# Attention and MLP on one core: batch 0 loaded in 1 KB pieces, queries kept in piece order, batch 1 loaded whole ahead of the weights

## The chip, the cores and the metric

The kernel runs on one core of a Trainium2 chip. The metric is the time of one execution on the device in microseconds (us). TensorE (PE), VectorE (DVE), ScalarE (ACT) and GpSimd (POOL) each have a queue of instructions of their own that they work off in order; SyncE (SP) here only issues DMA transfers. A DMA can also be issued from ScalarE's or GpSimd's queue, and then takes a place in that queue.

## The reference

```python
B, H, S, D = 8, 8, 576, 64
scores = scale * q @ k.T                      # per batch and head
cum = cumsum(maximum(s, 0.0))                 # per batch and head, over S
bias = minimum(-(cum[query] - cum[key]), 0.0)
scores = where(causal, -1e9, scores + bias)   # causal: key after query
attn = softmax(scores);  x = attn @ v         # x: [B, S, 512], the heads side by side
xn = (x - mean(x)) / sqrt(var(x) + 1e-6) * g_ln
out = x + maximum(xn @ w_ch1, 0.0) @ w_ch2    # 512 -> 2048 -> 512, all float32
```

## The kernel before

**Tiling.** The 576 tokens of a batch make four full blocks of 128 and a tail of 64 (`NF` = 4, `NT` = 5, `TL` = 64). A head's scores are computed transposed: keys on the partitions, queries along the row, one block of keys after the other and only the queries from that block on (`score_mms`). Blocks 0 and 1 go to the PSUM tile `s01`, blocks 2 and 3 to `s23`, block 4 to the end of the tile `pot`, of which there are two. ScalarE takes the exponential into `e` (`score_exp`); `values` multiplies `e` with V and a column of ones into `pot`, and VectorE divides by the sums into `x` (L272, L273). The causal mask is added by a matmul with `negm` for the first 12 heads (`NPM`), and applied by GpSimd to `e` after that (L236).

**Bias.** The cumulative sum enters the score matmul as four more rows of the contraction: `aug` holds, per token and head, 64 values of q or k, then the sum split into bf16 parts (`split`, `shift`). The sum is computed with tokens along the row and transposed by TensorE into `c8` (L502 to L508; `cum_quads` for batches in `QUADS`).

**Loads.** Batches 0 to 2 are loaded head by head in float32 (`head_in`, 128 KB each) into `homes`: those of q and k of batch 1 are `xbufs[0]`, where the cumulative sum is computed first, and the place of batch 0's q; that of v of batch 1 is the place of batch 0's k. A head is cast to bf16 into `aug` or `v_bf` (`cast_head`, called by `feed` four heads ahead), which frees its place. In batches of `QUADS` (1 and 2) partition p receives tokens 4p to 4p + 3 of q and k as one piece of 1 KB; in batch 0, and for v, a piece is one token of 256 bytes. The last 64 tokens of several heads come in one transfer (`tails_in`). From batch 3 on, `loads` brings token blocks through a ring.

**Transposes.** `t_pe` turns `aug` into `qkT` (68 rows, tokens along the row) by TensorE through PSUM tiles `pt`; `ps_m` has three such buffers, shared with the MLP's `ph` and `py`. For `QUADS`, `t_quads` transposes the pieces, and the copy from PSUM to `qkT` puts the tokens back into their order (L170 to L174), the tails of q and k in one copy of 128 after both (L175). From batch 3 on DMA transposes do this work.

**MLP.** When a batch is done, `stats`, `norm` and `x_t` normalize it, and `chunk_units` adds 32 units of work: 16 times up (4 matmuls into `ph`, ReLU into `hT` on ScalarE or VectorE) and 16 times down (4 matmuls; each fourth finishes 128 tokens of `py`, VectorE adds `x` into `yo`, and `store` puts the tile on the list `late`). `mlp(n)` runs up to n units; ahead of each it issues the stores of all tiles but the last on ScalarE's queue (L303). `yo` has two buffers.

**Order.** The program is written out for heads g = 0 to 63 in a loop of fixed places: "a", scores, "a2", exponentials and MLP units, "b", values of head g - 1, "x", "c", "d", "e". `at(g, place, f)` hangs work onto a place. The first MLP units run at head 11. W1 is loaded by four transfers on GpSimd's queue at heads 6, 6, 7, 7, W2 at 10, 10, 11, 11, both cast to bf16 on the way. The heads of batch 1 are issued on SP at heads 0, 0, 1, 1, 7, 7, 8, 8, those of batch 2 from head 12 on. `spin` issues matmuls whose result is not used.

Of the kernel before, what the change touches and what calls it, by code (L numbers as in the profile page):

```python
# [9 lines left out]
F32 = mybir.dt.float32  # L10
BF16 = mybir.dt.bfloat16
ALU = mybir.AluOpType
# [4 lines left out]
def kernel(  # L17
# [35 lines left out]

    QUADS = (1, 2)
    NPX = 2
# [17 lines left out]

    negm = const.tile([P, P], BF16, name="negm")
    nc.gpsimd.memset(negm, 0.0)
    nc.gpsimd.affine_select(
        out=negm, in_=negm, compare_op=ALU.is_ge, fill=-131072.0, base=0, pattern=[[1, P]],
        channel_multiplier=-1,
    )

# [16 lines left out]
    xnT_tail = const.tile([P, 2, KD, P], BF16, name="xnT_tail")  # L97

    scr = xbufs[0]
    ident_f = scr[:BH, 4:5, 64 : 64 + BH].rearrange("p a b -> p (a b)")  # L100
# [4 lines left out]

    nc.sync.dma_start(out=s_sb, in_=s.rearrange("b h s -> (b h) s"))


# [12 lines left out]
    def copy(eng, o, i):  # L121
        if eng == "act":
            nc.scalar.copy(out=o, in_=i)
        elif eng == "dve":
            nc.vector.tensor_copy(out=o, in_=i)  # L125
        else:
            nc.gpsimd.tensor_copy(out=o, in_=i)  # L127
# [33 lines left out]
    def t_quads(b, h, engs):  # L161
        pts = [ps_m.tile([P, 2 * 512], BF16, name="pt", tag="pm") for _ in range(2)]
        tails = pts[1][0:DK, NF * P : NF * P + 2 * P].rearrange("r (j n) -> r j n", j=2)
        for i in range(2):
            for p in range(NF):
                nc.tensor.transpose(  # L166
                    pts[i][0:DK, p * P : (p + 1) * P], aug[:, p, i * H + h, 0:DK], ident
                )
            nc.tensor.transpose(tails[:, i, :], aug[:, NF, i * H + h, 0:DK], ident)
            copy(  # L170
                engs[i],
                qkT[b][0:DK, i * H + h, 0 : NF * P].rearrange("r (p t) -> r p t", t=NF),
                pts[i][0:DK, 0 : NF * P].rearrange("r (t p) -> r p t", t=NF),
            )  # L174
        copy(  # L175
            "dve", qkT[b][0:DK, :, NF * P : S].rearrange("r (j h) n -> r j h n", j=2)[:, :, h, :],
            tails[:, :, 0:TL],
        )

    def t_pe(b, h, engs=("dve", "dve")):  # L180
        if b in QUADS:
            return t_quads(b, h, engs)
        for j, eng in ((h, engs[0]), (H + h, engs[1])):
            pt = ps_m.tile([P, 2 * 512], BF16, name="pt", tag="pm")
            for p in range(NT):
                nc.tensor.transpose(pt[0:DK, p * P : (p + 1) * P], aug[:, p, j, 0:DK], ident)
            copy(eng, qkT[b][0:DK, j, :], pt[0:DK, 0:SP_])

# [9 lines left out]
    def score_mms(g):  # L198
        b, h = g // H, g % H
        s01 = ps_s.tile([P, 1024], F32, name="s01", tag="s01")  # L200
        s23 = ps_s.tile([P, 512], F32, name="s23", tag="s23")
        pot = ps_o.tile([P, 512], F32, name="pot", tag="pot")
        pots[g] = (pot, s01, s23)

        def mm(o, kb, lo, hi):
            lhsT = qkT[b][0:DK, H + h, kb * P : (kb + 1) * P]
            w = 0
            if g < NPM and lo == kb * P:
                w = min(P, hi - lo)
                nc.tensor.matmul(  # L210
                    o[:, 0:w], lhsT=lhsT, rhs=qkT[b][0:DK, h, lo : lo + w], start=True, stop=False
                )
                nc.tensor.matmul(
                    o[:, 0:w], lhsT=ident, rhs=negm[:, 0:w], start=False, stop=True
                )
            if lo + w < hi:
                nc.tensor.matmul(  # L217
                    o[:, w:], lhsT=lhsT, rhs=qkT[b][0:DK, h, lo + w : hi], start=True, stop=True
                )

        mm(s01[:, 0:512], 0, 0, 512)
        mm(s01[:, 512:576], 0, 512, 576)
        mm(s01[:, 576:1024], 1, 128, 576)
        mm(s23[:, 0:320], 2, 256, 576)
        mm(s23[:, 320:512], 3, 384, 576)
        mm(pot[:, 448:512], 4, 512, 576)

    def score_exp(g, part):
        pot, s01, s23 = pots[g]
        e = ebufs[g % 3]  # L230

        def ex(o, i):
            nc.scalar.activation(out=o, in_=i, func=ACT.Exp, scale=scale)  # L233

        def mask(d):
            nc.gpsimd.affine_select(  # L236
                out=d, in_=d, compare_op=ALU.is_ge, fill=0.0, base=0,
                pattern=[[0, d.shape[1]], [1, P]], channel_multiplier=-1,
            )

        if part == 0:
            ex(e[:, 0:1024], s01)
        else:
            ex(e[:, EO[2] : EO[2] + 512], s23)
            ex(e[:, EO[4] : EO[4] + TL], pot[:, 448:512])
            if g >= NPM:
                mask(e[:, 0 : 3 * S].rearrange("p (n c) -> p n c", c=S)[:, :, 0:P])
                mask(
                    e[:, EO[4] + P - 448 : EO[3] + P]
                    .rearrange("p (n c) -> p n c", c=448)[:, :, 448 - P : 448]  # L250
                )

# [39 lines left out]
    def store(c, a, yo):  # L292
        if c >= B:
            b0 = 4 * (c - B) + 2 * a
            late.append((out[b0, NF * P : S, :], yo[0:TL]))
            late.append((out[b0 + 1, NF * P : S, :], yo[TL:P]))
        else:
            late.append((out[c, a * P : (a + 1) * P, :], yo))

    def stores(eng, keep=0):  # L300
        while len(late) > keep:
            o, i = late.pop(0)
            eng.dma_start(out=o, in_=i)  # L303

# [185 lines left out]
    def spin(n):  # L490
        for _ in range(n):
            nc.tensor.matmul(idle[:, 0:P], lhsT=ident, rhs=ident, start=True, stop=True)

    spin(44)
    nc.vector.tensor_scalar(
# [5 lines left out]
    )  # L501
    pc = ps_m.tile([P, 512], F32, name="pc", tag="pm")  # L502
    for p in range(NT):
        nc.tensor.transpose(pc[:, p * BH : (p + 1) * BH], cum[:, p * P : (p + 1) * P], ident_f)
    c8, r8 = (
        x[:, 0 : NT * BH].rearrange("p (t c) -> p t c", c=BH) for x in (xts[2], xts[1])
    )
    pc_v = pc[:, 0 : NT * BH].rearrange("p (t c) -> p t c", c=BH)  # L508

# [11 lines left out]
    cast_head("k", 0, 0, "pool")  # L521
    split(0, H, nc.vector, pc_v[:, :, 0:H], aug[:, :, H:HD, D1:DK])
    nc.scalar.activation(
# [3 lines left out]
    cast_head("k", 0, 1, "pool")  # L527
    spin(8)
    t_pe(0, 0, ("act", "dve"))
    nc.scalar.copy(out=c8, in_=pc_v)  # L530

    def cum_quads():

        pq = ps_m.tile([P, 512], F32, name="pq", tag="pm")[:, 0 : NF * 3 * H]
        pq = pq.rearrange("p (t c) -> p t c", t=NF)
        cum_q = cum[0 : 3 * H, 0 : NF * P].rearrange("c (p t) -> c t p", t=NF)
        for p in range(NF):
            nc.tensor.transpose(pq[:, p, :], cum_q[:, p, :], ident_f[0 : 3 * H, 0 : 3 * H])
        qs = slice(QUADS[0] * H, (QUADS[-1] + 1) * H)
        nc.vector.tensor_copy(out=c8[:, 0:NF, qs], in_=pq[:, :, qs])  # L540

# [10 lines left out]
    def at(g, pos, f):  # L552
        hooks.setdefault((g, pos), []).append(f)
# [13 lines left out]
    def t_next(g):  # L567
        t_pe((g + 2) // H, (g + 2) % H, ("dve", "act" if g >= H else "dve"))

    at(0, "a2", lambda: t_pe(0, 1))  # L570
    at(0, "a2", cum_quads)
    at(2, "c", lambda: split(H, 2 * H, nc.vector))
# [3 lines left out]
    for g in range(2 * H):  # L576
        if g < 12:
            at(g, "a", lambda g=g: feed(g))
        if g < 14:
            at(g, "a2" if g < H else "b", lambda g=g: t_next(g))  # L580
    for c, g in enumerate((6, 6, 7, 7)):
        at(g, "a", lambda c=c: load_w1(c))
# [6 lines left out]
    def b1_in(h):  # L589
        if h == 2:  # L590
            nc.sync.dma_start(out=gln_b, in_=moe_g_ln.partition_broadcast(P))
        heads_in(1, (h,))
        if h % HH == 0:
            for what in "qkv":
                tails_in(what, 1, nc.sync, slice(h, h + HH))

    for h, g in enumerate((0, 0, 1, 1, 7, 7, 8, 8)):
        at(g, "e", lambda h=h: b1_in(h))
# [6 lines left out]
    def t_act(b, h):  # L605
        t_pe(b, h, ("dve", "act"))

# [18 lines left out]
    at(10, "c", lambda: chunk_units(0))  # L626
    for i, g in enumerate((10, 10, 11, 11)):
        at(g, "b", lambda i=i: load_w2(i))
    for p in (1, 2, 3, 4):
        at(6 + p, "e", lambda p=p: nc.gpsimd.memset(aug[:, p, :, DK:P], 0.0))  # L630


    def b2_in(g):
        if g == 12:
            for what in "qkv":
                tails_in(what, 2, nc.sync)
        heads_in(2, range(3 * (g - 12), min(H, 3 * (g - 12) + 3)))

    for g in (12, 13, 14):
        at(g, "a", lambda g=g: b2_in(g))  # L640
# [62 lines left out]
    for g in range(NG + 4):  # L703
# [7 lines left out]
        if g < NG:  # L711
            score_mms(g)
            run(g, "a2")
            score_exp(g, 0)
        mlp(min(1, nu))
# [44 lines left out]
```

The softmax here doesn't subtract the row's maximum and nothing guards it: scores larger than these inputs give would overflow.

## Time and profile before

| what | value |
|---|---|
| median of 13 runs | 378.66 us |
| lowest, highest | 377.45, 381.04 us |
| profiled execution: its own time | 378.0 us |
| profiled execution: span of its instructions | 376.3 us |
| granted TensorE clock | 0.999 |
| bytes moved by DMA | 59.12 MB |
| first MLP matmul (`ph`) starts at | 42.9 us |
| exponential of head 0, 8, 16 starts at | 10.4, 30.2, 80.3 us |

The profile is that of one execution, 0.66 us below the median. Times inside it count from the start of the span. A group's row names the line, engine, operation, output and input with their shapes, and the count, then the busy time in us and the mean of one in ns, then the idle time of the engine just before and what ended it. A row of the waits names the waiting work, what ended the wait, the total in us, how often, and the longest.

### The profile page before, as it was taken

To read this page: it belongs to the slowest core of one execution; us is meant where nothing else is said; L and a number is where in the kernel's file an instruction comes from. 1 tells how busy PE (TensorE), PEld (TensorE's weight loads), DVE (VectorE), ACT (ScalarE), POOL (GpSimd) and SP (SyncE) were. 2 spreads that over 40 slices of the span, in tenths; PEclk is the share of its full clock that TensorE was granted. 3 is DMA by queue.
4 is the path that set the end of the run, shared out by engine and by line. 5 is a ranking of instruction groups with operands and counts; after the bars stand their busy time and mean duration, and the time that the engine had idled before them with its cause. 6 is when DMAs were issued, how large, how long until landed. Compare 5 with 4: busy or idle time off the path is not lost.

```text
span 376.3 us, 7905 instructions
## 1 busy us (share of the span) xinstructions
PE 352.6 (94%) x2991; PEld 204.1 (54%) x3017; DVE 200.7 (53%) x466; ACT 164.1 (44%) x295; POOL 167.8 (45%) x328
## 2 busy tenths in 40 slices
PE   7977879798999999999999999999999999899994
PEld 6866545365555455555555755555555555344471
DVE  6789565754455434594447335723555453933131
ACT  3666665154651476336632546434633563031020
POOL 3647973592635546475446444463444111600000
PEclk9999999999999999999999999999999999999999
DMA  9978989997999399999999999699604001420202
GB/s 164 212 187 183 216 146 207 247 240 158 209 217 250 83 213 204 228 207 195 191 200 254 178 246 212 128 214 214 118 28 113 29 2 56 113 56 0 86 28 56
DMA packets 175254, 59.12 MB, mean 157 GB/s; under 512 B 162225, under 2 KB 170417, under 8 KB 175217
## 3 DMA queue, kind: packets, MB, share of 16 engines
q1 hardware_dynamic: 165200, 46.43, 64.1%
q0 software_dynamic: 4224, 4.19, 6.9%
q10 hardware_dynamic: 5792, 8.00, 6.4%
q8 instruction: 23, 0.38, 0.4%
q14 instruction: 15, 0.11, 0.1%
HBM read 37.11 MB, written 9.44 MB: 124 GB/s over the span
## 4 chain that ended last, share of the span: by engine, by line
PE 74%; DMA 10%; DVE 6%; SPq 4%; issue 2%; POOL 1%; ACT 1%; POOLq 0%; DVEq 0%; ACTq 0%
PE ph L373 29%; PE py L384 27%; PE s L217 9%; PE pot L264 6%; DMA ring<-in_k_dram 4%; DMA ring<-in_q_dram 4%; SPq L430 2%; DVE xn L323 2%; DVE stats L308 1%; SPq L434 1%; DMA xnT<-xn 1%; SPq L422 1%; DVE x L273 1%; PE pt L166 1%; DMA out_dram<-yo 1%
## 5 line engine op out<-in xcount | busy, mean ns | idle before, releaser
L233 ACT ACTIVATE e<-s 128x1024 bf16<-128x1024 f32 (+1 forms) x128 | 99.1, 808 | 87.4 <-PE s L217 83.8
L384 PE MATMUL py<-w_bf,hT 128*128 128x512 bf16 x550 | 129.8, 379 | 1.4
L373 PE MATMUL ph<-xnT,w_bf 128*128 128x512 bf16 x512 | 120.7, 379 | 1.7 <-DMA xnT<-xn 1.7
L236 POOL TENSOR_SCALAR_AFFINE_SELECT e<-e 128x384 bf16<-128x384 bf16 x104 | 45.9, 466 | 111.2 <-ACT e L233 102.7
L358 DVE TENSOR_SCALAR hT<-ph 128x512 bf16<-128x512 f32 x72 | 49.7, 691 | 76.6 <-PE ph L373 76.0
L373 PEld LDWEIGHTS <-w_bf 128*128 128x128 bf16 x640 | 58.2, 98 | 50.2 <-issue 2.2
L384 PEld LDWEIGHTS <-hT 128*128 128x128 bf16 x576 | 53.1, 98 | 56.1 <-DVE hT L358 0.2
L356 ACT ACTIVATE hT<-ph 128x512 bf16<-128x512 f32 x72 | 43.0, 597 | 79.9 <-PE ph L373 77.7
L217 PE MATMUL s<-qkT 68*128 68x64 bf16 (+5 forms) x320 | 54.0, 286 | 0.0
L127 POOL CAST aug<-ring 128x512 bf16<-128x512 f32 (+2 forms) x85 | 45.3, 558 | 13.8 <-DMA ring<-in_k_dram 11.8
L390 DVE SCALAR_TENSOR_TENSOR yo<-py,rstd,x 128x512 f32<-128x512 f32 x32 | 24.0, 749 | 47.2 <-PE py L384 45.0
L217 PEld LDWEIGHTS <-qkT 68*128 68x128 bf16 x372 | 32.3, 98 | 24.6
L264 PEld LDWEIGHTS <-e 128*128 128x128 bf16 x960 | 37.4, 98 | 14.3 <-POOL e L236 1.5
L264 PE MATMUL pot<-v_bf,e 128*128 128x65 bf16 x960 | 39.7, 193 | 2.2 <-POOL e L236 1.4
L273 DVE TENSOR_TENSOR x<-pot,rinv 128x320 f32<-128x320 f32 x64 | 31.5, 492 | 2.9 <-DMA out_dram<-yo 0.6
L125 DVE COPY qkT<-pt 68x512 bf16<-68x512 bf16 (+2 forms) x49 | 21.8, 468 | 11.4 <-PE pt L166 4.4
L308 DVE BATCH_NORM_STATS2 stats<-x 128x6 f32<-128x256 f32 (+2 forms) x68 | 23.4, 399 | 0.3
L323 DVE SCALAR_TENSOR_TENSOR xn<-x,mv,gln_b 128x512 bf16<-128x512 f32 x32 | 23.2, 766 | 0.0
L272 DVE RECIPROCAL rinv<-pot 128x5 f32<-128x5 f32 x64 | 12.0, 188 | 15.3 <-PE pot L264 15.3
L127 POOL CAST v_bf<-ring 128x512 bf16<-128x512 f32 (+2 forms) x33 | 19.3, 606 | 1.9 <-DMA ring<-in_v_dram 1.9
L329 POOL TENSOR_TENSOR rstd<-rstd,nhalf 128x2 f32<-128x2 f32 x18 | 18.2, 1012 | 1.5
L328 POOL TENSOR_SCALAR rstd<-mv 128x2 f32<-128x2 f32 x18 | 10.1, 560 | 11.9 <-DVE mv L319 11.7
(78 smaller groups left out, 218.4 us busy)
## 6 DMA issues: line engine op xcount, KB each, us to landing
out_dram<-yo ACTq DMA_DIRECT2D x27, 256.0 KB, 3.3
ring<-in_q_dram SPq DMA_DIRECT2D x20, 256.0 KB, 4.7
ring<-in_k_dram SPq DMA_DIRECT2D x20, 256.0 KB, 5.1
ring<-in_v_dram SPq DMA_DIRECT2D x20, 256.0 KB, 4.1
w_bf<-in_moe_w_ch_dram POOLq DMA_DIRECT2D x8, 512.0 KB, 9.3
ring<-in_k_dram SPq DMA_DIRECT2D x30, 128.0 KB, 4.3
ring<-in_q_dram SPq DMA_DIRECT2D x22, 128.0 KB, 4.4
x<-in_v_dram SPq DMA_DIRECT2D x17, 128.0 KB, 4.2
```

Source lines behind the costliest of these rows:

```text
L127: nc.gpsimd.tensor_copy(out=o, in_=i)
L217: nc.tensor.matmul(o[:, w:], lhsT=lhsT, rhs=qkT[b][0:DK, h, lo + w : hi], start=True, stop=True)
L233: nc.scalar.activation(out=o, in_=i, func=ACT.Exp, scale=scale)
L236: nc.gpsimd.affine_select(out=d, in_=d, compare_op=ALU.is_ge, fill=0.0, base=0, pattern=[[0, d.shape[1]], [1, P]], channel_multiplier=-1,)
L264: nc.tensor.matmul(pot[:, t * D1 : (t + 1) * D1], lhsT=e[:, c : c + P], rhs=v_bfs[b % 2][:, kb, h, :], start=(kb == 0), stop=(kb == t),)
L273: nc.vector.tensor_tensor(out=xs[b][:, :, h * D : (h + 1) * D], in0=pv[:, :, 0:D], in1=rv.to_broadcast([P, NT, D]), op=ALU.mult,)
L308: nc.vector.bn_stats(out=sts[c, a][:, part, :], in_=x_of(c, a)[:, lo:hi])
L323: eng.scalar_tensor_tensor(out=xn[:, j, :], in0=x_of(c, a), scalar=mv[:, j, 0:1], in1=gln_b, op0=ALU.subtract, op1=ALU.mult,)
L356: nc.scalar.activation(out=o, in_=i, func=ACT.Relu)
L358: nc.vector.tensor_scalar_max(out=o, in0=i, scalar1=0.0)
L373: nc.tensor.matmul(ph[:, j * tok : (j + 1) * tok], lhsT=w1_bf[:, kd, fb * P : (fb + 1) * P], rhs=xnT[c][:, :, kd, :], start=(kd == 0), sto ...
L384: nc.tensor.matmul(st["py"], lhsT=st["h"][:, fb, a * P : (a + 1) * P], rhs=w2_bf[:, fb, :], start=(fb == 0), stop=(fb == FB - 1),)
```

## The change

Batch 0 joins `QUADS`. The key copies still restore the order of the tokens, but the queries stay as they were transposed: four runs of 128 in `qkT`, and a block of 128 queries is read as four runs of 32. So the scores, `e`, `x` and `yo` of a full tile have token 4p + t at place 32t + p, the mask for such blocks has that order (`negq`, and a pattern in `mask`), and a tile is stored by four transfers of 32 rows. The tail of 64 tokens keeps its order. Score matmuls are cut at query 512, where the order changes. Block 4 of the scores is issued after the place "a2". The cumulative sum of batches 0 to 2 is transposed first, in piece order (`pq`), that of the others at head 1 (`cum_all`). The row of g_ln is loaded once on GpSimd's queue and spread over the partitions by a matmul at head 3 (`spread_g`). All heads of batch 1 are issued at heads 1 and 3; W1 is issued at heads 7, 7, 8, 8, W2 at 9, 9, 10, 10. `spin` issues a quarter as many matmuls of four times the width.

```diff
-    QUADS = (1, 2)
+    QUADS = (0, 1, 2)
+    QN, QP = 4, 32
...
+    negq = const.tile([P, P], BF16, name="negq")
...
     nc.sync.dma_start(out=s_sb, in_=s.rearrange("b h s -> (b h) s"))
+    nc.gpsimd.dma_start(out=gln_r, in_=moe_g_ln.rearrange("(o f) -> o f", o=1))
+    nc.gpsimd.memset(ones_r, 1.0)
...
     def t_quads(b, h, engs):
...
         for i in range(2):
+            pt = ps_m.tile([P, 2 * 512], BF16, name="pt", tag="pm")
+            o = qkT[b][0:DK, i * H + h, :]
+            for p in range(NT):
                 nc.tensor.transpose(
+                    pt[0:DK, p * P : (p + 1) * P], aug[:, p, i * H + h, 0:DK], ident
                 )
+            if i == 0:
+                copy(engs[0], o[:, 0:S], pt[0:DK, 0:S])
+            else:
+                copy(
+                    engs[1], o[:, 0 : NF * P].rearrange("r (p t) -> r p t", t=NF),
+                    pt[0:DK, 0 : NF * P].rearrange("r (t p) -> r p t", t=NF),
+                )
+                copy(engs[2], o[:, NF * P : S], pt[0:DK, NF * P : S])
...
+        def queries(lo, hi):
+            qT = qkT[b][0:DK, h, :]
+            if b in QUADS and hi <= NF * P:
+                qT = qT[:, 0 : NF * P].rearrange("r (t a p) -> r a t p", t=QN, p=QP)
+                return qT[:, lo // P : hi // P]
+            return qT[:, lo:hi]
...
+            cuts = {lo, hi}
+            if b in QUADS and lo < NF * P:
+                cuts.add(min(hi, NF * P))
             if g < NPM and lo == kb * P:
+                cuts.add(min(hi, lo + P))
+            cuts = sorted(cuts)
+            for c0, c1 in zip(cuts[:-1], cuts[1:]):
...
-        mm(pot[:, 448:512], 4, 512, 576)
+        return lambda: mm(pot[:, 448:512], 4, 512, 576)
...
             if g >= NPM:
                 mask(e[:, 0 : 3 * S].rearrange("p (n c) -> p n c", c=S)[:, :, 0:P])
+                if g // H in QUADS:
+                    for c, w in ((EO[3], P), (EO[4], TL)):
+                        mask(e[:, c : c + w].rearrange("p (n c) -> p n c", n=1))
...
-            late.append((out[c, a * P : (a + 1) * P, :], yo))
+            o = out[c, a * P : (a + 1) * P, :]
+            if c in QUADS:
+                o = o.rearrange("(q t) f -> t q f", t=QN)
+                late.append([(o[t], yo[t * QP : (t + 1) * QP]) for t in range(QN)])
...
-    spin(44)
+    spin(11)
...
-    t_pe(0, 0, ("act", "dve"))
-    nc.scalar.copy(out=c8, in_=pc_v)
+    t_quads(0, 0, ("act", "dve", "act"))
+    nc.scalar.copy(out=c8[:, :, 0:NQ], in_=pq)
...
+    def spread_g():
+        pg = ps_m.tile([P, 512], F32, name="pg", tag="pm")
+        nc.tensor.matmul(pg, lhsT=ones_r, rhs=gln_r, start=True, stop=True)
+        nc.vector.tensor_copy(out=gln_b, in_=pg)
...
-        t_pe((g + 2) // H, (g + 2) % H, ("dve", "act" if g >= H else "dve"))
+        t_quads((g + 2) // H, (g + 2) % H, ("dve", "act" if g >= H else "dve", "dve"))
...
-    at(0, "a2", cum_quads)
+    at(1, "c", cum_all)
+    at(3, "c", spread_g)
...
-    for c, g in enumerate((6, 6, 7, 7)):
+    for c, g in enumerate((7, 7, 8, 8)):
         at(g, "a", lambda c=c: load_w1(c))
...
-        if h == 2:
-            nc.sync.dma_start(out=gln_b, in_=moe_g_ln.partition_broadcast(P))
...
-    for h, g in enumerate((0, 0, 1, 1, 7, 7, 8, 8)):
+    for h, g in enumerate((1, 1, 1, 1, 3, 3, 3, 3)):
         at(g, "e", lambda h=h: b1_in(h))
...
-    for i, g in enumerate((10, 10, 11, 11)):
+    for i, g in enumerate((9, 9, 10, 10)):
         at(g, "b", lambda i=i: load_w2(i))
...
-            score_mms(g)
+            score_tail = score_mms(g)
             run(g, "a2")
+            score_tail()
             score_exp(g, 0)
```

## The prediction

> **What bounds the kernel now.** I read the page first, then the busy time of each engine in stretches of the span, then the waits of TensorE and the chain that ended last, last the groups with each shape apart.
>
> ```profile
> span 376.3 us, 7905 instructions
> PE 352.6 (94%) x2991; PEld 204.1 (54%) x3017; DVE 200.7 (53%) x466; ACT 164.1 (44%) x295; POOL 167.8 (45%) x328
> ```
>
> TensorE is busy for 94% of the span, so the average says little; the stages say more (columns: stretch, length, then busy time of PE, PEld, DVE, ACT, POOL, then clock, DMA share, GB/s).
>
> ```profile
> 20.00:30.00 10.00, 8.19 (x156) 7.34 (x157) 8.12 (x23) 6.08 (x12) 4.10 (x10) 1.00 0.72 191
> 30.00:40.00 10.00, 6.76 (x105) 5.25 (x104) 9.73 (x29) 6.58 (x12) 9.03 (x14) 1.00 0.94 182
> 50.00:60.00 10.00, 8.12 (x72) 4.44 (x69) 7.46 (x19) 5.20 (x11) 7.43 (x13) 1.00 0.95 146
> 70.00:80.00 10.00, 6.80 (x64) 4.35 (x64) 7.58 (x18) 3.66 (x7) 8.97 (x18) 1.00 0.94 232
> 80.00:90.00 10.00, 8.59 (x89) 5.64 (x88) 5.87 (x14) 5.79 (x11) 4.82 (x12) 1.00 1.04 241
> 150.00:200.00 50.00, 49.68 (x397) 26.63 (x402) 28.65 (x66) 21.06 (x38) 26.23 (x50) 1.00 1.12 209
> ```
>
> From 90 to 340 us TensorE is full: time saved before that moves the end one for one, and matmul time added there lengthens it one for one. Everything to win lies in the first 90 us. There no single resource is full. Between 30 and 40 us VectorE (9.73 of 10) and GpSimd (9.03) are; the DMA engines are not (0.72 between 20 and 30 us). What TensorE waits for between 16 and 60 us (total, times, longest):
>
> ```profile
> PE pot L210 <- DVE x L273: 3.1, 5, 1.1
> PE pot L264 <- POOL e L236: 1.4, 1, 1.4
> PE pt L166 <- POOL aug L127: 1.3, 2, 1.0
> PE pot L264 <- POOL v_bf L127: 0.8, 2, 0.5
> PE pt L166 <- DVE hT L358: 0.5, 1, 0.5
> ```
>
> The first row is block 4 of the scores waiting for the `pot` buffer that VectorE empties; the other three large ones are GpSimd being late with casts and masks. The chain says why it is late (start, length, what):
>
> ```profile
> 25.46 5.37 DMA ring<-in_k_dram
> ...
> 38.65 11.45 DMA ring<-in_k_dram
> ...
> 59.09 9.05 DMA ring<-in_q_dram
> ...
> 68.57 0.68 DVE hT L358
> ```
>
> Three loads carry it: keys of batch 1 that land late for GpSimd's casts (30.8 and 50.1 us), and a query head of batch 2 that lands at 68.1, behind the second half of the weights. For the latter VectorE idles 1.1 and 0.8 us ahead of two casts (L125), with `hT` and the values of head 15 queued behind it.
>
> **What the Trainium skill says.** DMA: Bandwidth & Descriptors, "Why small descriptors are slow": a 256-byte descriptor carries a fixed overhead of some 27%. The trace agrees in kind: 216 GB/s while only 256-byte pieces move (4 to 17 us), 263 to 321 GB/s in the slices where pieces of 1 KB and more prevail (27 to 29 us). VectorE: DVE Perf Modes, "Why PSUM operands drop a tier": a bf16 copy out of PSUM reaches twice the base rate at most, and Advanced Engine Details and Errata, "Mode Summary", asks unit stride for it. The rows agree (the last two columns before the idle time: busy, mean ns):
>
> ```profile
> L125 DVE COPY qkT<-pt 68x512 bf16<-68x512 bf16 x18 | 12.1, 680 | 4.5 <-PE pt L166 4.4
> L125 DVE COPY qkT<-pt 68x640 bf16<-68x640 bf16 x15 | 6.7, 481 | 4.1 <-PE pt L186 4.0
> L125 DVE COPY qkT<-pt 68x128 bf16<-68x128 bf16 x16 | 3.5, 217 | 2.8 <-ACT qkT L123 2.8
> ```
>
> 640 elements straight are cheaper than 512 reordered. TensorE: Matmul & The Clock Gate, "Back-to-back issue gap", gives about 25 ns as the least distance of two small matmuls; here 15 matmuls of 65 columns take 0.455 us, 30 ns each.
>
> **The change, part by part.** The sum is made against the profiled execution, 378.0 us (span 376.3 and 1.7 around it); the median of 13 runs is 0.66 above it.
>
> Loads of batch 0 (q and k, 16 x 128 KB): 2.1 MB at 216 GB/s is 9.7 us, at 300 it is 7.0, and SP's issue falls from 0.54 to 0.43 us each. The first head hardly gains: its transposes (7.92) wait for the chain scan, five transposes, splits (3.7 to 7.9 us), not for data. The first key copy becomes a reordered one, 0.68 instead of 0.48: **+0.2**. What the loads do buy is SP time: batch 1's first heads can be issued about 3 us earlier than 18.0, heads 4 to 7 from about 24 instead of 31 us, all ahead of the weights. GpSimd's waits for loads and releases (3.0, 2.0, 1.9, 1.4 us) then mostly go.
>
> VectorE up to head 10. Batch 0 now costs per head a straight copy of 576 (about 0.45, from 481 for 640), a reordered one of 512 (0.68) and a tail of 64 (about 0.2), overlapped about 1.22 instead of 0.88 for a pair: 0.34 x 7 = 2.4. The copy of g_ln out of PSUM is new, 128x512 f32, 0.65 to 0.69 by `hT` L358: 0.65. The `cum` copy costs 0.1 more. Batches 1 and 2 save: 1.40 becomes 1.15 in two heads, and about 0.3 in each of three where ScalarE has the key copy: -1.4. Together +1.8 on an engine nearly full. Against it: block 4 now follows the transposes, so these no longer stand behind the 3.1 us of waits for `pot`, nor VectorE behind them (its gaps of 0.61 ahead of L125 at 16.0, 20.9 and 23.0 us, and 0.56 at 28.8): -2.4. GpSimd is on time with casts, of 1.3 + 0.8 us I count -1.5. Two `xn` pairs that take 1.61 and 2.00 us beside a busy GpSimd instead of 1.40: half, -0.4. The first MLP matmul (42.9 us) thus comes at about 40.4: **-2.5**, ends 0 and -5.
>
> After that, all weights are issued from GpSimd before the casts of head 11, which adds 1.5 us there, against some 8 us of waits gone: those casts end about 47 instead of 53.9 us. The stalls of 1.4 (mask) and 0.5 us (54 to 56 us) go: **-1.4** (0 to -1.9). Batch 2's loads wait in SP for these same casts (13.2 us at L422); issued 7 us earlier, and behind weights that are 10 us earlier too, heads 0 and 1 land around 60 us, when VectorE gets to them: **-1.5** of 1.9. What is late next is VectorE's own chain of values, statistics and `xn`. In batch 2's transposes the tail copy no longer follows ScalarE's key copy (2.8 us of such waits) and the query copy is shorter; TensorE waited 1.8 us there: **-0.5** (0 to -1.5).
>
> Added matmuls: blocks 1 and 2 gain one piece each in 12 heads, block 3 too in the 12 after. Columns stay equal, so a piece costs its fixed part, 3 to 30 ns; of 60 about 38 lie where TensorE is full: **+0.4** (0 to 1.1). The queries are read in runs of 32 elements, which the trace does not show; `xnT` is read in runs of 128 at 216 ns for 512 columns. SBUF — State Buffer, "Door 1", speaks of 16-byte lines that want two hits; a run of 32 has eight on each. I take 0. At half rate 13 heads x 1280 columns / 2.4 GHz = 6.9 us would be the upper end; a gain is excluded, as `qkT` was read straight before.
>
> Stores: 12 tiles x 3 more issues x 0.338 us (L303) is 12.2 us on ScalarE's queue, 44% busy. They fall in the down half, where ScalarE has no ReLU; an `e` behind them is needed a head later. The last of four is issued 1.0 us later, and `yo` has two buffers: VectorE may wait. I take **+0.8** (0 to 4, if ten tiles each cost 0.4). Without that cover it is up to 12.2. The masks of heads 12 to 23 in two instructions (about 0.5 instead of 0.41), the memsets, the g_ln row on GpSimd's queue (one issue, under 1 us while GpSimd idles from 3.2 to 7.0) and five `cum` transposes at head 1 in place of four at head 0 cost nothing on the path while GpSimd has a head of slack and VectorE is behind TensorE; g_ln's matmul, some 0.9 us, lies beside VectorE's splits. All that, uncovered, is 1 to 2 us. The eleven wide idle matmuls have the columns of the 44: nothing.
>
> Sum: +0.2 - 2.5 - 1.4 - 1.5 - 0.5 + 0.4 + 0.8 = -4.5, so 373.5 for this execution, **374.2** against the median.
>
> **The rivals.** *The loads are hidden anyway.* For it: up to 28 us VectorE and TensorE set the pace, not data. Then only the stall at 54 to 56 us and part of the query wait go, about -2.4 + 1.2 - 0.3: 377. *VectorE becomes the bound of the first ten heads*, which ends slower: its +1.8 is paid in full since it has no idle time left, the moved block 4 saves nothing as its buffer and the transposes' three PSUM buffers are all emptied by VectorE, and the later waits stay since everything shifts: +0.2 + 1.8 + 0.4 + 0.8 = +3.2, 381.9. It decides once the gaps removed ahead of L125 are under 1.8 us. For it: 9.73 of 10 at 30 to 40 us; against: 2.4 us of gaps released by TensorE. *The reading in pieces or the stores cost TensorE time* in heads 11 to 23: +4 to +9 on the forecast, 378 to 383. That the change does nothing at all cannot be: the copies and stores differ.
>
> **How the numbers follow.** Forecast 0.55 (372 to 377), of a larger gain 0.03, loads hidden 0.15 (two thirds of it faster, the rest even), VectorE 0.15, pieces or stores 0.12 (a quarter even). About 0.3%, 1.1 us, is what a measurement of this kernel tells from no change. Taking some chance off the forecast for the many parts that must all hold: faster 0.62, same 0.12, slower 0.26. The range 370.5 to 381.5 leaves out the largest gains and the dearest pieces; the forecast's own is 371.5 to 377.
>
> **What would show it.** The first `ph` matmul near 40 us, casts of head 11 done near 47, no VectorE wait for batch 2's loads, L125 rows of 576 near 0.45 us, TensorE above 9.3 of 10 between 50 and 60 us, and score matmuls of 256 columns spaced as columns / 2.4 GHz. The forecast is wrong if `ph` starts after 42.9, if score pieces take longer than their columns, or if `yo` or `e` wait behind L303.

## The result and the profile after

The changed kernel is **slower**, by some 1%: 383.47 us, the median of 11 runs (379.67 to 385.45), against 378.43 us for the kernel before in the same session. Two of the 11 runs, of 385.45 us each, fell in a slower state, so the ratio leaves them out, and the experiments are compared with the median of the other nine, 382.73 us. The ratio is 1.0109, its 95% interval 1.0088 to 1.0131. The forecast was 374.2 us, with a range of 370.5 to 381.5. The profiled execution took 380.64 us by itself, with a span of 378.7; it is 2.1 us below that median, so its stalls are probably smaller than usual.

From the head of the page of the changed kernel:

```profile
span 378.7 us, 8031 instructions
PE 355.9 (94%) x3014; PEld 205.2 (54%) x3041; DVE 197.3 (52%) x474; ACT 163.6 (43%) x296; POOL 171.6 (45%) x345
```

The shares are nearly those of before; the averages hide the loss. The stretches of the changed kernel show it (stretch, length, busy time of PE, PEld, DVE, ACT, POOL, then clock, DMA share, GB/s):

```profile
30.00:40.00 10.00, 7.39 (x151) 6.57 (x149) 9.41 (x33) 7.47 (x15) 8.69 (x14) 1.00 1.11 189
50.00:60.00 10.00, 9.69 (x95) 5.48 (x91) 8.05 (x21) 5.84 (x11) 5.46 (x15) 1.00 1.23 207
70.00:80.00 10.00, 8.91 (x90) 6.00 (x88) 5.05 (x13) 5.61 (x10) 9.92 (x25) 1.00 0.94 226
120.00:130.00 10.00, 7.63 (x40) 4.17 (x41) 3.72 (x8) 3.98 (x7) 2.53 (x5) 0.83 0.33 75
```

The last of these stretches in the kernel before:

```profile
120.00:130.00 10.00, 9.15 (x55) 4.51 (x55) 6.11 (x15) 3.97 (x7) 5.56 (x10) 1.00 0.56 130
```

Up to 90 us the forecast holds in direction: TensorE is busier in each of the first three stretches shown than it was before (6.76, 8.12 and 6.80). The exponential of head 16 starts at 76.53 us where it started at 80.33, that of head 19 at 93.65 against 97.30. Some 3.7 us are won. Then, between 120 and 130 us, where TensorE was to be full, it is busy for 7.63 us of 10 at a clock of 0.83. What happens there is on ScalarE's queue (start, length, what; in brackets the idle time before and its releaser):

```profile
112.24 0.32 ACTq L325 DMA_DIRECT2D out_dram<-yo  x1
113.57 8.33 ACTq L325 DMA_DIRECT2D out_dram<-yo  x7
121.94 0.59 ACT L131 COPY xnT<-ptx 128x512 bf16<-128x512 bf16 x1 [8.62 <-DMA out_dram<-yo]
```

These are the stores of two tiles, from units of the MLP between which ScalarE has no other work. One issue takes 0.32 to 0.43 us once it starts. The first starts at 112.24, the others at 113.57, 114.68, 117.06, 118.52, 118.88, 121.10 and 121.46. So seven stores hold the queue for 8.33 us, not for 7 x 0.338 = 2.4: most of it is time between the issues. Behind them stands the copy of `xnT` (L131). VectorE in turn may not write the next `yo` before the stores of the buffer have landed, and TensorE's next transposes wait for VectorE. TensorE's timeline, the changed kernel:

```profile
118.64 0.39 PE L362 MATMUL ptx<-ident,xn 128*128 128x128 bf16 x4
122.14 0.58 PE L362 MATMUL ptx<-ident,xn 128*128 128x128 bf16 x4 [3.12 <-DVE yo L412]
...
126.17 0.82 PE L220 MATMUL s<-qkT 68*128 68x512 bf16 x5
```

What the stores wait for stands in the chain of work that ended last (start, length, what):

```profile
111.98 5.06 DMA ring<-in_q_dram
117.04 0.02 issue
117.06 4.20 DMA out_dram<-yo
121.26 0.03 DVEq L412
121.29 0.04 issue
121.34 0.76 DVE yo L412
122.10 0.04 issue
122.14 0.58 PE ptx L362 x4
```

A load that SP issued at 111.98 lands at 117.04, and only then does the store start. The issues at 113.57, 114.68, 118.52 and 121.10 follow the landing of a load by 0.02 to 0.08 us in the same way. The trace names the semaphore (a counter that a DMA raises when it lands) of every transfer: those of SP and ScalarE share eight semaphores in strict turn, and none of the 265 that take a semaphore over was issued before the transfer that had it eight places earlier had landed. So this program never has more than eight of them under way, and a store waits for a load that has nothing to do with it.

TensorE stands still for 3.12 us and then runs at a mean clock of 0.57 from 122 to 126 us; at half rate it runs from 122.11 to 125.52, for 3.41 us. The Trainium skill (TensorE: Matmul & The Clock Gate, Part 1) says that the clock falls to half after an idle window of some 3.4 us and needs a busy one to come back. The trace agrees with the half rate and with how long it lasts, but 3.12 us without a matmul were enough here. So a stall of 3 us costs somewhat more than 3 us.

### The profile page after: what moved, and what is told of

It is laid out like the page before. It is cut to its first block, busy times and chain, and to the rows that moved or that the text cites. A ratio compares the mean times of both kernels' runs of the same rounds, so it can differ in the third digit from the quotient of the medians.

```text
span 378.7 us, 8031 instructions
## 1 busy us (share of the span) xinstructions
PE 355.9 (94%) x3014; PEld 205.2 (54%) x3041; DVE 197.3 (52%) x474; ACT 163.6 (43%) x296; POOL 171.6 (45%) x345
## 4 chain that ended last, share of the span: by engine, by line
PE 66%; DMA 14%; POOL 5%; DVE 5%; issue 4%; SPq 3%; ACT 1%; ACTq 0%; DVEq 0%; POOLq 0%
PE ph L395 26%; PE py L406 22%; PE s L220 8%; PE pot L280 5%; DMA ring<-in_v_dram 4%; DMA x<-in_v_dram 3%; DMA ring<-in_q_dram 3%; DMA ring<-in_k_dram 2%; DMA out_dram<-yo 2%; POOL aug L135 2%; PE pt L174 2%; PE idle L514 1%; SPq L187 1%; POOL e L248 1%; DVE xn L345 1%
## 5 line engine op out<-in xcount | busy, mean ns | idle before, releaser
L248 POOL TENSOR_SCALAR_AFFINE_SELECT e<-e 128x384 bf16<-128x384 bf16 (+2 forms) x116 | 48.3, 441 | 109.7 <-ACT e L240 101.2
L378 ACT ACTIVATE hT<-ph 128x512 bf16<-128x512 f32 x72 | 42.9, 597 | 80.3 <-PE ph L395 79.8
L220 PEld LDWEIGHTS <-qkT 68*128 68x128 bf16 x492 | 41.0, 100 | 32.3 <-DVE x L289 4.7
L220 PE MATMUL s<-qkT 68*128 68x64 bf16 (+7 forms) x428 | 57.2, 266 | 0.9 <-DVE qkT L133 0.8
L133 DVE COPY qkT<-pt 68x576 bf16<-68x576 bf16 (+2 forms) x56 | 19.6, 380 | 14.9 <-PE pt L174 8.9
L174 PE MATMUL pt<-ident,aug 128*68 128x128 bf16 x240 | 19.2, 230 | 2.4 <-DVE qkT L133 1.2
L351 POOL TENSOR_TENSOR rstd<-rstd,nhalf 128x2 f32<-128x2 f32 x18 | 19.0, 1056 | 1.5
L135 POOL CAST v_bf<-ring 128x512 bf16<-128x512 f32 (+2 forms) x33 | 18.3, 577 | 2.4 <-DMA ring<-in_v_dram 2.4
```

Of the source, the lines that this page charges most:

```text
L220: nc.tensor.matmul(d, lhsT=lhsT, rhs=queries(c0, c1), start=True, stop=not m)
L248: nc.gpsimd.affine_select(out=d, in_=d, compare_op=ALU.is_ge, fill=0.0, base=0, pattern=pattern, channel_multiplier=-1,)
L378: nc.scalar.activation(out=o, in_=i, func=ACT.Relu)
```

## The experiments

The theories: **stores** (36 more transfers cost up to 10 us, in bursts, and everything else gains what was forecast); **clock** (the wide idle matmuls leave TensorE at half clock at the start: the profile has 0.50 from 9.5 to 16.3 us); **first heads** (the queries in pieces or VectorE cost what the loads save). All ratios below are to the kernel before in the same session, with 95% intervals.

### One store a tile

```diff
-            if c in QUADS:
-                o = o.rearrange("(q t) f -> t q f", t=QN)
-                late.append([(o[t], yo[t * QP : (t + 1) * QP]) for t in range(QN)])
-            else:
-                late.append([(o, yo)])
+            late.append([(o, yo)])
```

> The changed kernel, but each full tile of batches 0 to 2 goes out in one transfer again, so its tokens lie in piece order in the output: the restoring of their order is left out. Theory (stores): the four transfers a tile hold ScalarE's queue (8.3 us for seven issues at 113.6 us, 7.3 us for five at 157.2) and TensorE stands behind it; without them the gain of some 4 us that stands at 97 us is kept: 373 to 375.5 us, ratio to before 0.985 to 0.992, no wait of ScalarE on L325. Rival (clock): the half clock of 9.7 to 16.3 us and later is what costs; then it stays above 381. Rival (early stage): VectorE's extra copies; then 378 to 380.

373.62 us, 0.986 (0.9829 to 0.9891). That is some 9 us below the changed kernel: 382.73 - 373.62 = 9.1 by the medians, 9.4 by the ratios. ScalarE's queue at the same place:

```profile
113.21 0.34 ACTq L321 DMA_DIRECT2D out_dram<-yo  x1
118.74 1.18 ACT L131 COPY xnT<-ptx 128x512 bf16<-128x512 bf16 x2 [5.75 <-PE ptx L358]
```

The copies now wait for TensorE alone. No store of this kernel starts within 0.1 us of the landing of the transfer whose semaphore it takes over; in the changed kernel 13 do. The TensorE timeline of one_store from the same pair of transposes on:

```profile
118.32 0.39 PE L358 MATMUL ptx<-ident,xn 128*128 128x128 bf16 x4
118.91 0.38 PE L358 MATMUL ptx<-ident,xn 128*128 128x128 bf16 x4 [0.21 <-DVE yo L408]
...
122.23 0.82 PE L220 MATMUL s<-qkT 68*128 68x512 bf16 x5
```

At the first line the two kernels are 0.3 us apart, at the score matmuls 3.94. This one burst costs 3.6 us; another, five stores in 7.25 us, starts at 157.18. Over the whole span the changed kernel has 378.7 - 355.9 = 22.8 us without a matmul, this one 371.8 - 354.2 = 17.6.

### Four stores in the kernel before

```diff
-            late.append((out[c, a * P : (a + 1) * P, :], yo))
+            n = P // 4 if c < 3 else P
+            late.append([
+                (out[c, r + a * P : r + a * P + n, :], yo[r : r + n]) for r in range(0, P, n)
+            ])
```

The two halves of a tail tile also become one entry of the list `late`, as in the changed kernel.

> The kernel before, with each full tile of batches 0 to 2 stored by four transfers of 32 rows in the usual token order; nothing else differs. Theory (stores): the cost is that of the issues and comes alone too, 5 to 10 us more than before: 383.5 to 388, bursts of over 5 us on ScalarE's queue. Rivals (clock, early stage): within 1 us of before, 377.5 to 379.5.

386.14 us, 1.0195 (1.0155 to 1.0235): +7.3 us from the stores alone. The instructions that have `yo` as operand, and who waited for the stores (engine, line, us in all, times):

```profile
L307 ACTq DMA_DIRECT2D out_dram<-yo x67: 321/366/1486, 80.1 to 333.8; - x67
...
  ACT e L233: 15.6, 4
  DVE yo L394: 9.4, 2
  ACT xnT L123: 8.5, 1
```

The row says why the price was easy to miss: the median issue is 366 ns. The loss is in the waiting rows, not in the duration; 17 of its stores start within 0.1 us of such a landing, against two in the kernel before.

### Narrow idle matmuls

```diff
-            nc.tensor.matmul(
-                idle, lhsT=ident,
-                rhs=ident.rearrange("p (o n) -> p o n", o=1).to_broadcast([P, 4, P]),
...
+            nc.tensor.matmul(idle[:, 0:P], lhsT=ident, rhs=ident, start=True, stop=True)
...
-    spin(11)
+    spin(44)
```

> The changed kernel with the idle matmuls of before, 44 and 8 of 128 columns instead of 11 and 2 of 512. Theory (stores): the clock at the start hardly matters to the end, since the lost 3 us are taken back by the waits that follow: 382 to 384, at most 1.5 us better. Rival (clock): half the clock from 9.7 to 16.3 us is the effect of the wide idle matmuls and costs 3 us: 380 to 381, with the clock at 1.00 from 8 to 16 us.

381.8 us, 1.0088 (1.0061 to 1.0115), an interval that overlaps that of the changed kernel. Its profile has the full clock between 10 and 20 us, but so has that of one_store with its wide idle matmuls, and before_four_stores with narrow ones has 0.66. The width does not set it. Nor does it matter: the exponential of head 16 starts at 76.53 us in the changed kernel and in one_store, at 76.50 here. The clock at the start falls as an explanation.

### Two stores per unit of the MLP

```diff
-    def stores(eng, keep=0):
-        while len(late) > keep:
-            for o, i in late.pop(0):
-                eng.dma_start(out=o, in_=i)
+    def stores(eng, keep=0, n=1000):
+        while len(late) > keep and n > 0:
+            o, i = late[0].pop(0)
+            eng.dma_start(out=o, in_=i)
+            n -= 1
+            if not late[0]:
+                late.pop(0)
...
-            stores(eng or nc.scalar, 0 if eng else 1)
+            stores(eng or nc.scalar, 0 if eng else 1, 1000 if eng else 2)
```

> The changed kernel, with at most two of the four transfers of a tile issued ahead of one MLP unit, so that other work of ScalarE comes in between. Theory (stores): bursts of eight become bursts of at most four to eight with reliefs, so a part comes back: 377 to 381. If the cost is the number of issues and not their bursts, it stays at 383; if the last store of a tile then lands too late for the yo buffer, VectorE waits and it is above 384.

381.06 us, 1.0062 (1.0038 to 1.0085): some 1.8 us by the ratios (1.7 by the medians) of the 9.1 come back. The burst at 114 us stays, seven stores in 8.23 us, since ScalarE has no other work between these units. A pair issued later takes 0.80 us. Spreading by units is not spreading in time.

### Queries put into order like the keys

```diff
-            if i == 0:
-                copy(engs[0], o[:, 0:S], pt[0:DK, 0:S])
-            else:
-                copy(
-                    engs[1], ...
-                copy(engs[2], ...
+            copy(
+                engs[i], o[:, 0 : NF * P].rearrange("r (p t) -> r p t", t=NF),
+                pt[0:DK, 0 : NF * P].rearrange("r (t p) -> r p t", t=NF),
+            )
+            copy(engs[2], o[:, NF * P : S], pt[0:DK, NF * P : S])
...
-            if b in QUADS and lo < NF * P:
-                cuts.add(min(hi, NF * P))
...
+            late.append([(o, yo)])
```

The masks go back to the order of the tokens with it.

> The changed kernel, but the query copy from PSUM restores the order of the tokens as the key copy does (512 reordered, a tail of 64), so the scores, masks and tiles are in token order and each tile goes out in one transfer; loads, order of work and g_ln stay as changed. The output is the reference's. Theory (stores): the four stores were the whole loss, and VectorE's dearer query copy (0.68 + 0.2 instead of 0.46 us) costs 0 to 1.5 us of the gain: 373.5 to 376, faster than both kernels. Rival (VectorE bounds the first ten heads): the copies cost 0.4 us in each of 16 heads in full, 378 to 381.

375.9 us, 0.9913 (0.9883 to 0.9943). It is **faster than both kernels**, than the one before by some 0.9%. It pays for the order in VectorE's copies; copies between PSUM and `qkT` of the changed kernel, by shape:

```profile
L133 DVE COPY qkT<-pt 68x576 bf16<-68x576 bf16 x23 | 10.3, 448 | 8.4 <-PE pt L174 8.2
L133 DVE COPY qkT<-pt 68x512 bf16<-68x512 bf16 x10 | 6.8, 680 | 0.7 <-PE pt L174 0.6
```

and of this one:

```profile
L133 DVE COPY qkT<-pt 68x512 bf16<-68x512 bf16 x33 | 22.5, 681 | 9.0 <-PE pt L174 9.0
L133 DVE COPY qkT<-pt 68x64 bf16<-68x64 bf16 x46 | 7.8, 179 | 0.9
```

23 x (681 + 179 - 448) ns = 9.5 us more of VectorE, of which about 2 reach the end (375.9 - 373.62 = 2.3; 2.0 by the ratios, whose intervals overlap a little). The 36 added stores, 12.2 us of issuing at 0.338 us each, cost some 9 us, though ScalarE too has idle time (43% busy). Copying is the cheaper place for the order: it adds work to a queue, but no transfers whose turn has to come.

### Stores on GpSimd's queue

```diff
-            for o, i in late.pop(0):
-                eng.dma_start(out=o, in_=i)
+            ps = late.pop(0)
+            for o, i in ps:
+                (nc.gpsimd if len(ps) == QN else eng).dma_start(out=o, in_=i)
```

> The changed kernel, with the four transfers of a tile issued on GpSimd's queue in place of ScalarE's. Theory (stores): what hurts is that exponentials and copies stand behind the issues in ScalarE's queue; on GpSimd they stand ahead of casts and masks, at 0.75 us each by the weight loads 3 us a tile, with a head of slack: 376 to 381. Rival (the transfers themselves, with 32 rows each, land too slowly for the two yo buffers): 382 or more whichever queue issues them.

391.1 us, 1.0326 (1.0287 to 1.0364), a worse place for them than ScalarE's queue. From the instructions with `yo` as operand:

```profile
L326 POOL DMA_DIRECT2D out_dram<-yo x48: 496/498/632, 78.8 to 209.2; - x48
...
  DMA out_dram<-yo: 26.9, 7
```

The issues are even, 0.5 us each, 2.0 for four: GpSimd's transfers take turns on eight semaphores of their own, and none of these stores waited for a load in this way. But they stand behind GpSimd's other work (those at 128.40 right behind the `rstd` of the normalization), and VectorE sat idle ahead of `yo` for 26.9 us, seven times, until stores had landed. ScalarE's queue being free does not help if `yo` waits.

### One transfer with a pattern of three dimensions

```diff
-                late.append([(o[t], yo[t * QP : (t + 1) * QP]) for t in range(QN)])
+                late.append([(o, yo)])
```

Here `o` remains the pattern of 4 x 32 x 512 in DRAM, so the one transfer puts the tokens into order itself.

> The changed kernel with its queries in piece order, but each tile stored by one transfer whose DRAM side is a pattern of 4 x 32 rows of 512 and whose source is the whole tile of 128 rows; the output is the reference's if the rows pair up as written. Theory (what costs is that one tile needs four issues): as one_store, 373 to 376, faster than both kernels. Rival (the scattered rows of 2 KB at a distance of 8 KB, or a transfer on fewer engines, land too slowly for the two yo buffers): VectorE waits for stores, 378 or more.

396.09 us, 1.0471 (1.0435 to 1.0507). The issue is short, yet VectorE waits for the buffer (its waits, then its timeline):

```profile
DVE yo L412 <- DMA out_dram<-yo: 21.6, 6, 5.8
```

```profile
132.43 0.75 DVE L412 SCALAR_TENSOR_TENSOR yo<-py,rstd,x 128x512 f32<-128x512 f32 x1 [5.81 <-DMA out_dram<-yo]
```

The store of that buffer was issued at 124.71. The Trainium skill (DMA: Bandwidth & Descriptors, "Why a DMA increments its semaphore by 16 and not by 1") says that a transfer runs on the largest number of engines up to 16 that divides the slowest dimension of both sides: for 4 and 128 that would be 4. The trace agrees: the store of 124.71 landed at 132.34, 7.6 us later (a median of 2.9 in one_store), and each of the twelve stores of this form raised its semaphore at five moments, every other store of ScalarE and SP at sixteen.

### The load order of before

On top of one_store, for the weights and the last four heads of batch 1; its first four stay at head 1:

```diff
-    for c, g in enumerate((7, 7, 8, 8)):
+    for c, g in enumerate((6, 6, 7, 7)):
...
-    for h, g in enumerate((1, 1, 1, 1, 3, 3, 3, 3)):
+    for h, g in enumerate((1, 1, 1, 1, 7, 7, 8, 8)):
...
-    for i, g in enumerate((9, 9, 10, 10)):
+    for i, g in enumerate((10, 10, 11, 11)):
```

> As one_store (one transfer a tile, token order of full tiles of batches 0 to 2 left out), but with the load order of before: the last four heads of batch 1 at heads 7, 7, 8, 8, W1 at 6, 6, 7, 7, W2 at 10, 10, 11, 11. Theory: loading batch 1 ahead of the weights gives most of the early gain, by GpSimd's casts being on time and batch 2's loads starting earlier; without it 376 to 378. Rival (the gain is from the 1 KB pieces of batch 0 and block 4's place): within 1 us of one_store, 373 to 374.5.

376.16 us, 0.994 (0.9911 to 0.9969), 2.5 us above one_store by the medians, 3.0 by the ratios. The wait of VectorE for batch 2's query heads is back (casts into `aug`, in an execution of 378.66 us, 2.5 above this kernel's median):

```profile
65.42 0.49 DVE L133 CAST aug<-ring 128x320 bf16<-128x320 f32 x1 [1.26 <-DMA ring<-in_q_dram]
68.03 0.48 DVE L133 CAST aug<-ring 128x320 bf16<-128x320 f32 x1 [2.12 <-DMA ring<-in_q_dram]
```

In the changed kernel the same two casts follow each other without a wait (in one_store the second waits for 0.17 us):

```profile
64.00 0.87 DVE L133 CAST aug<-ring 128x320 bf16<-128x320 f32 x2
```

### Batch 0 in pieces of 256 bytes

On top of one_store, in `head_in`; this kernel leaves out that the tokens of batch 0 then stand in another order than its cumulative sum:

```diff
-        if b in QUADS and what != "v":
+        if b in QUADS and b > 0 and what != "v":
```

> As one_store, but q and k of batch 0 are loaded in pieces of 256 bytes as before (their tokens then stand in another order than the cumulative sum's, which is not mended). Theory: the pieces buy some 3 us of SP and DMA time in the first 20 us, which the later heads of batch 1 get; 0.5 to 2 us slower than one_store, 374 to 376. Rival (loads of batch 0 are hidden, VectorE and TensorE set the pace to 28 us): no difference, within 0.7 us of one_store.

376.39 us, 0.9949 (0.993 to 0.9968), 2.8 us above one_store by the medians, 3.4 by the ratios. Again the casts of batch 2 wait, 1.57 and 0.47 us, and head 16's exponential starts at 78.23 instead of 76.53. So the size of the pieces in batch 0 tells some fifty microseconds later, at the loads of batch 2. Whether the first heads gain as well, these profiles do not show, since their clocks differ there.

### Block 4 of the scores in its old place

On top of one_store:

```diff
-            score_tail = score_mms(g)
+            score_mms(g)()
...
-            score_tail()
```

> As one_store (token order of full tiles of batches 0 to 2 left out), but block 4 of the scores is issued ahead of the place a2 again, as in the kernel before. By the prediction its move is worth 2.4 us at the first MLP matmul: 375 to 376.5. Rival (the batch 2 loads, due at the same time anyway, set the pace to 76 us): within 0.7 us of one_store, 373 to 374.5.

374.69 us, 0.9907 (0.9883 to 0.9931): 1.1 us above one_store by the medians, 1.8 by the ratios, with intervals that overlap slightly. A small gain of the move is likely, not certain.

### Queries read element by element

The copies are straight, and TensorE reads the queries in token order with a distance of 128 elements; single stores and token-order masks:

```diff
-                qT = qT[:, 0 : NF * P].rearrange("r (t a p) -> r a t p", t=QN, p=QP)
-                return qT[:, lo // P : hi // P]
+                qT = qT[:, 0 : NF * P].rearrange("r (t p) -> r p t", t=QN)
+                return qT[:, lo // QN : hi // QN]
```

> The changed kernel with the straight query copy, but the score matmuls read the queries element by element in token order (32 x n places, four elements at a distance of 128), so masks, tiles and single stores are in token order. It prices the reading: the run of 32 elements cost nothing in the trace of the changed kernel. If TensorE reads scattered elements at full rate: 373 to 375. If at half rate: 13 heads x 1280 columns are 6.9 us more where TensorE is full, 380 to 382; at a quarter, 390 or more. I expect half rate.

412.51 us, 1.0899 (1.0856 to 1.0941). The score matmuls of the changed kernel, in runs of 32, and of this one:

```profile
L220 PE MATMUL s<-qkT 68*128 68x384 bf16 x24 | 8.2, 342 | 0.0
```

```profile
L220 PE MATMUL s<-qkT 68*128 68x384 bf16 x24 | 19.6, 816 | 0.0
```

(816 - 342) / 384 = 1.23 ns more a column. 24 heads x 1280 columns x 1.23 ns = 37.9 us; the difference to one_store is 38.9. Runs of 32 elements cost nothing: a set of scores of a head takes 0.82 us in eight pieces, and took 0.82 in five straight ones before.

### Four stores by columns in the kernel before

```diff
-            late.append((out[c, a * P : (a + 1) * P, :], yo))
+            n = Dm // 4 if c < 3 else Dm
+            late.append([
+                (out[c, a * P : (a + 1) * P, f : f + n], yo[:, f : f + n]) for f in range(0, Dm, n)
+            ])
```

> The kernel before, with each full tile of batches 0 to 2 stored by four transfers of 128 rows by 128 columns (512 bytes a row) in place of one. Against before_four_stores (386.1, four of 32 rows) it tells the count of issues from their shape. Theory (count: each further issue makes ScalarE wait some 1 us while SP issues loads): again 384 to 389. Rival (32 rows, two to a DMA engine, are what is slow): 378 to 381.

382.45 us, 1.0109 (1.0068 to 1.015): +4.0 us for the same count and bytes over all 128 partitions, where pieces of 32 rows cost +7.3. So the count alone costs, and 14 stores of this kernel start within 0.1 us of such a landing. The shape of 32 rows costs more, and why is open.

## Why the prediction was wrong

**The step that failed is the stores**, "+0.8 (0 to 4 ...)". They measured some 9 us in the changed kernel (9.1 by the medians, 9.4 by the ratios) and 7.3 in the kernel before. Three things in it were wrong.

- The unit price. 0.338 us is one issue that follows no other, as in the kernel before. In the burst most issues came 1.1 to 2.4 us apart. The uncovered figure, 12.2, was thus no upper bound for ScalarE's time in itself: the burst at 113.57 alone held the queue for 8.33 us with 7 of 36 + 12 issues. The prediction put at nothing what a store waits for before it is issued: the landing of the transfer eight places ahead of it, at that time mostly a load of 256 KB, at a DMA share of 1.17. In one_store no store was held up by such a landing. No run changed the number of semaphores, so this share of the price is read from the trace; that the added stores cost, the runs with and without them show. SP's own issues are long there too, up to 1.42 us, but as long in one_store (up to 1.55, DMA share 1.19), and why is open.
- The cover. "In the down half, where ScalarE has no ReLU" left out the copies of `xnT`, and that ScalarE has nothing else to do between the stores of two tiles, so that eight stores meet. "An `e` behind them is needed a head later" holds for one tile's stores of 1.4 us, not for 8.
- The wait for `yo`, named but not priced: TensorE's 3.12 us, and the clock after it.

**The early gains held as a sum, in part by luck.** All terms but the stores came to -5.3 us; one_store measured 373.62 against 378.8, which is -5.2. But single terms were off, and their errors cancel: the mask stall stayed, and the loads of batch 2 were worth more.

- *First MLP matmul, 42.9 to 40.4, -2.5.* It started at 42.96 in the profile of the changed kernel, whose TensorE ran at half clock from 9.5 to 16.3 us, at 40.99 in one_store (half clock from 36.3 to 39.7) and at 40.21 in spin_narrow (full clock up to there, as in the kernel before). So the time as forecast came about where the clock was that of the kernel before. Its parts did not: TensorE's waits for `pot` between 16 and 60 us stayed, with 2.6 us in the changed kernel and 3.0 in one_store instead of 3.1, as block 4 still wants the buffer wherever it stands. At the end of the span moving it is worth 1.1 to 1.8 us by block4_before, not 2.4.
- *Casts of head 11 done at 47, mask stall -1.4.* They were done at 52.8, since a load of v issued at 36.93 landed only at 52.25 (the one before it, issued at 33.25, at 46.95). The stall is absent in the changed kernel's stretch from 50 to 60 us (PE 9.69) and there in one_store's (8.04, with 1.5 us of waits for GpSimd's masks), which is the faster one: it is not what the gain rests on, and the term of -1.4 did not come.
- *VectorE's wait for batch 2's loads, -1.5.* Right, and the largest in truth: undoing the order of the loads costs 2.5 to 3.0 us, undoing the pieces of batch 0 2.8 to 3.4, and both bring this wait back. The two cannot be added, since each alone makes the same heads late.
- *Copies and reading.* Straight copies of 576 took 448 ns (about 450 forecast). Reading in runs of 32 cost 0, as taken, and added pieces 0 instead of +0.4. The skill's lines of 16 bytes (SBUF — State Buffer, "Door 1") are in accord with both ends: runs of 64 bytes free, single elements at about a quarter of the rate, a figure that the page does not give.

Of the rivals, "the reading in pieces or the stores cost TensorE time", at 378 to 383, was the one that came, in its second half; its chance was 0.12, and the measured 382.7 to 383.5 us lies at its upper end. VectorE as the bound did not come: its copies were 9.5 us heavier still in queries_in_order, for about 2 us.

## What to carry to other kernels

Price an added DMA issue by what its queue does in that stage: how many stores can fall together, how many transfers the program allows under way at once and which one must land before the next may start (here eight, shared by two queues), what stands behind the stores, and when the buffer is free again. The duration of a single issue is only the lower end. If tokens must be put back into order, do it where data is copied anyway and the engine has idle time (here VectorE, 2 us), not by splitting the store (some 9 us), and keep a store one transfer over all 128 partitions. A saving that a trace shows early must be followed to the end of the span, since a stall of 3 us far behind it can take it all back.

## What the runs showed of the hardware that was not expected

- Seven stores in a row from ScalarE took 8.2 to 8.4 us in three kernels while SP was issuing loads; a pair later took 0.80. Most of it (5.6 of 8.33 us in the changed kernel) was waiting for loads to land, since this program's transfers from both queues share eight semaphores. A median of issue durations (428 ns) does not show it.
- Four stores of 32 partitions cost 7.3 us in all, four of 128 columns 4.0, for the same bytes. From GpSimd's queue an issue is an even 0.5 us.
- Storing twelve tiles with a leading DRAM dimension of 4 cost 22 us more than plain stores (396.09 against 373.62), with waits of up to 5.8 us for the buffer. Each of these stores raised its semaphore at five moments instead of sixteen.
- TensorE read its moving operand in runs of 32 bf16 elements at full rate, and in single elements at a distance of 128 at 1.64 ns a column: 1.23 more than the 0.41 of straight rows (192 columns in 246 ns, 448 in 351).
- TensorE had half its clock for 3.4 us or a multiple of it (6.8 in the changed kernel) near the start in some profiles and not in others, with wide and narrow idle matmuls alike, and by head 16 the difference was gone (76.53 and 76.50 us). The skill's page on the clock gate (Part 1) speaks of a window that runs free of the kernel's start, which would fit.
